# LayerNorm and two matmuls with GELU on one core: three first tiles transposed raw, their mean and deviation applied afterwards

## The chip, the core and the metric

One core of a Trainium2 chip runs the kernel. The metric is the device time of one execution in microseconds (us), median of several runs; the kernel before takes 398.55 us (three runs, 398.34 to 398.63). TensorE (PE) multiplies 128x128 blocks of weights with up to 512 columns and writes to PSUM, eight banks of 512 float columns; VectorE (DVE), ScalarE (ACT) and GpSimd (POOL) work elementwise; the DMA queues used here are issued from SyncE (SP) and ScalarE.

## The reference

```
def _layernorm(x, axis=-1, eps=1e-5):
    m = jnp.mean(x, axis=axis, keepdims=True)
    v = jnp.var(x, axis=axis, keepdims=True)
    return (x - m) / jnp.sqrt(v + eps)

def reference(x, w1, b1, w2, b2):
    y = _layernorm(x, axis=-1)
    h = _gelu(jnp.einsum("bsd,df->bsf", y, w1) + b1)
    return jnp.einsum("bsf,fd->bsd", h, w2) + b2
```

x is (1, 2048, 1024), w1 (1024, 3584), w2 (3584, 1024), all bfloat16; GELU is the tanh form. There is no scale or shift in the normalisation.

## The kernel before

**Tiling.** The 2048 tokens are four blocks of 512, each of four tiles of 128 tokens. A token tile comes with tokens on the partitions; for the first matmul it has to lie the other way (`yT_sb`, 128 features on the partitions, eight of them for 1024 features, index `dt`). The first matmul makes for each of 28 rows of 128 hidden features (index `r`) a PSUM bank of 128x512 from eight matmuls of 512 columns; ScalarE adds b1 and takes GELU into `hT_sb` (`act_gelu`, L430). The second matmul (`out_chunk`, L453) makes 128 tokens x 512 outputs from 28 matmuls; VectorE adds b2 (L477) and SyncE stores. Per block, all 28 rows of the first matmul run, then the eight chunks of the second.

**Order of work.** Each engine's instructions are written out by hand in its own list (`_Prog`), with waits on named events; only VectorE's list behind the head is merged by a small planner at the end (L569 to L584), from due times that are estimates in the source. `ring` (L393) gives the PSUM banks: row 7 uses bank `t`, row 8 the bank of row 0, and so on, so row 8 waits for the GELU of row 0.

**The first block.** Its weights are not there yet: w1's first 896 columns (seven rows) come in eight chunks, one for each `dt`, w0 to w7, mixed with the token tiles in `SP_FIRST_LOADS` (L32) and `ACT_FIRST_LOADS` (L33). So the first seven rows are a "wave": seven banks are open at once (`wave`, L505), and matmuls of 128 columns, one token tile at a time, follow the loads in an order that L508 to L522 write out. TensorE itself transposes the tiles of this block (`pe_T`, L367): a transpose through the identity into bank `t` or a bank not yet in use, then a copy by ScalarE (L385). From block 1 on VectorE transposes (L355).

**Normalising the first block.** VectorE takes batch statistics (L264) and aggregates them (L271); POOL makes 1/deviation by a power (L268). Tiles 2 and 3 are normalised in full ahead of their transposes (L290). Tiles 0 and 1 (`N_CENTRED`) are only centred: tile 0 from a mean that VectorE and ScalarE take half each (L494, L275, L281), tile 1 by L286. Their deviation is applied later to each PSUM bank of this block, 256 columns, by `dve_scale` (L423 to L428), with `rbc_sb`, the two tiles' deviations laid along the columns by sixteen small VectorE transposes (L337).

**Warm-up.** 37 matmuls of a constant (`warm`, L488) run while the first loads come, the last three of them behind tile 0's mean; three more follow its first transposes.

Of the kernel before, what the change touches and what calls it, by code (L numbers as in the profile page):

```python
# [6 lines left out]
ALU = mybir.AluOpType  # L7
# [8 lines left out]
K_GROUPS = 2  # L16
# [4 lines left out]
WARM_A = ((34, None), (3, "m4"))  # L21
WARM_B = 3
N_CENTRED = 2
T_PUTS = {0: (None, None, 6), 1: (21, 35), 2: (96, 118), 3: (140, 156)}
NORM = {0: (0, 2, 8), 1: (0, 4, 8), 2: (0, 4, 8)}
GROUPS_0 = (0, 2, 5, 8)
WAVE_ROWS_0 = 6
WAVE_K = (0, 2, 4, 5, 6, 8)
GROUPS_1 = (0, 4, 8)
W1_CHUNK_COLS = (512, 512, 1024, 640)  # L30
N_W2_CHUNKS = 4
SP_FIRST_LOADS = ("x0a", "w0", "w1", "w2", "w3", "w4", "w5", "x2a", "x2b", "w6", "w7", "x3a", "x3b", "b1", "w8")  # L32
ACT_FIRST_LOADS = ("x0b", "x1")  # L33

T_PE_START = 5.7
T_DVE_START = 16.5
# [54 lines left out]
def bass_standalone__mixer_channel_mlp__prompt_kernel(  # L91
# [22 lines left out]
    nkg = max(1, min(K_GROUPS, DT))  # L114
    KGROUPS = [(h * DT // nkg, (h + 1) * DT // nkg) for h in range(nkg)]
    assert NB1 + NB2 + 1 <= 8 and NB2 == 2
    assert all(c[-1] == DT for c in (*NORM.values(), GROUPS_0, GROUPS_1, WAVE_K))
# [27 lines left out]
    with ExitStack() as es:  # L145
# [19 lines left out]
        half_sb = sb("half_sb", [P, 1], F32)  # L165
        m4_sb = sb("m4_sb", [P, 1], F32)
        rq_sb = sb("rq_sb", [P, N_CENTRED, 32], F32)
        rbc_sb = sb("rbc_sb", [P, N_CENTRED, P], F32)

# [4 lines left out]
        ps_tf = ps_t[:, :, :].bitcast(F32)  # L174

# [37 lines left out]
        def issue(item):  # L213
            if item[0] == "x" and item[-1] in "ab":
                i, h = int(item[1:-1]), "ab".index(item[-1])
                dma(x_sb[:, i, h * HC:(h + 1) * HC], xf[i * P:(i + 1) * P, h * HC:(h + 1) * HC], f"x{i}_{h}",
                    P * HC * 2)
                x_ev[i] = (f"x{i}_0", f"x{i}_1")
            elif item == "b1":
                b1v = b1.rearrange("(t q a) -> q t a", q=4, a=32)  # L220
                for q in range(4):
                    dma(b1r_sb[32 * q:32 * q + FT, :], b1v[q], f"b1{q}", F // 2, waits=["b1z"])
            elif item[0] == "x":
                load_x_tile(int(item[1:]))
            elif item[0] == "w" and int(item[1:]) < len(w1_chunks):
                load_w1(int(item[1:]))
# [32 lines left out]
        pool.op(lambda e: e.memset(b1r_sb[:, :], 0.0), sig="b1z")  # L259
        dve.op(lambda e: e.memset(st_sb[:, :, 12:14], 0.0))  # L260
# [6 lines left out]
        def op_aggr(i):  # L267
            pool.op(lambda e, i=i: e.tensor_tensor(out=rstd_sb[:, i:i + 1], in0=mv_sb[:, i, 1:2],  # L268
                                                   in1=nhalf[:, i:i + 1], op=ALU.pow),
                    waits=[f"mv{i}", "nhalf"], sig=f"rstd{i}")  # L270
# [3 lines left out]
        def op_mean0():  # L274
            return (lambda e: e.tensor_scalar(out=m4_sb[:, :], in0=st_sb[:, 0, 1:2], scalar1=st_sb[:, 0, 4:5],  # L275
                                              scalar2=half_sb[:, :], op0=ALU.add, op1=ALU.add),
                    ["st0_0", "half"], "m4", 0.1)

        def op_norm(i, c0, c1, sig):
            if i == 0:  # L280
                return (lambda e, c0=c0, c1=c1: e.tensor_scalar(  # L281
                            out=o_sb[:, 0, c0:c1], in0=x_sb[:, 0, c0:c1], scalar1=4.0,
                            scalar2=m4_sb[:, :], op0=ALU.mult, op1=ALU.subtract),
                        ["m4"], sig, 0.02 + (c1 - c0) * 0.00055)
            if i < N_CENTRED:
                return (lambda e, i=i, c0=c0, c1=c1: e.tensor_scalar(  # L286
                            out=x_sb[:, i, c0:c1], in0=x_sb[:, i, c0:c1], scalar1=mv_sb[:, i, 0:1],
                            scalar2=None, op0=ALU.subtract),
                        [f"mv{i}"], sig, 0.02 + (c1 - c0) * 0.00055)
# [7 lines left out]
        def ops_norm(i):  # L297
            cuts = NORM.get(i, (0, DT))
# [27 lines left out]
        def ops_rbc():  # L326
            res = []
            for i in range(N_CENTRED):
                res.append((lambda e, i=i: e.tensor_scalar(out=rq_sb[:, i, :], in0=ones[:, 0:32],
                                                           scalar1=rstd_sb[:, i:i + 1], scalar2=(1.0 if i else 0.25),  # L330
                                                           op0=ALU.mult, op1=ALU.mult),
                            ["ones", f"rstd{i}"], f"rq{i}", 0.1))
            for tq in range(4):
                for q in range(4):
                    src = rq_sb[32 * tq:32 * (tq + 1), :, :]
                    dst = rbc_sb[32 * q:32 * (q + 1), :, 32 * tq:32 * (tq + 1)]
                    res.append((lambda e, src=src, dst=dst: e.transpose(out=dst, in_=src), [f"rq{N_CENTRED - 1}"],  # L337
                                ("rbc" if tq == 3 and q == 3 else None), 0.1))
            return res
# [4 lines left out]
        def ops_T(i):  # L344
            blk, t = divmod(i, TPB)
            waits = [y_ev[i][-1]]
            if blk - 2 in mm1_done:
                waits.append(mm1_done[blk - 2])
            res = []
# [15 lines left out]
        t_banks = [("t", ps_t[:, 0, :]), ("2_0", ps_2b[:, 0, :]), ("t", ps_t[:, 0, :])]  # L365

        def pe_T(i, groups, k):  # L367
            blk, t = divmod(i, TPB)
            j0, j1 = groups[k], groups[k + 1]
            bname, bap = t_banks[k if i == 0 else 0]  # L370
            evs = yT_ev.setdefault(i, [None] * DT)
            for j in range(j0, j1):
                waits = []
                if j == j0:
                    waits = ["ident"] + ([bank_read[bname]] if bname in bank_read else [])
                if j == j0 or y_ev[i][j] != y_ev[i][j - 1]:
                    waits.append(y_ev[i][j])
                pe.op(lambda e, i=i, j=j, o=(j - j0) * P, bap=bap: e.transpose(  # L378
                    out=bap[:, o:o + P], in_=(x_sb[:, i] if i else o_sb[:, 0])[:, j * P:(j + 1) * P],
                    identity=ident[:, :]),  # L380
                    waits=waits, sig=(f"tp{i}_{k}" if j == j1 - 1 else None))
                evs[j] = f"te{i}_{k}"
            src = bap[:, 0:(j1 - j0) * P].rearrange("p (j s) -> p j s", j=j1 - j0)
            dst = yT_sb[:, blk % 2, j0:j1, t * P:(t + 1) * P]
            act.op(lambda e, dst=dst, src=src: e.copy(out=dst, in_=src), waits=[f"tp{i}_{k}"], sig=f"te{i}_{k}")  # L385
            bank_read[bname] = f"te{i}_{k}"
            pe_t[0] += (j1 - j0) * 0.056
# [20 lines left out]
        def pe_cell(b, r, t0, t1, bank, waits, sig, dts=None, opens=True, closes=True):  # L408
            n0, n1 = t0 * P, t1 * P
            dts = list(range(DT)) if dts is None else list(dts)  # L410
            waits = list(waits)
            for k, dt in enumerate(dts):
                w = (waits if k == 0 else []) + [f"w1c{w1_chunk_of(r, dt)}"]
                w += [yT_ev[b * TPB + t][dt] for t in range(t0, t1)]
                pe.op(lambda e, b=b, r=r, dt=dt, n0=n0, n1=n1, bank=bank: e.matmul(  # L415
                    unit_bank(bank)[:, n0:n1], lhsT=w1_sb[:, dt, r * P:(r + 1) * P], rhs=yT_sb[:, b % 2, dt, n0:n1],
                    start=(opens and dt == 0), stop=(closes and dt == DT - 1)),
                    waits=w, sig=(sig if dt == DT - 1 else None))
            pe_t[0] += len(dts) * _mm_us(n1 - n0)
            if dts[-1] == DT - 1:  # L420
                est[sig] = pe_t[0]

        def dve_scale(r, bank, wait_ev):  # L423
            ap = unit_bank(bank)[:, 0:N_CENTRED * P]
            crit.append((est[wait_ev], (lambda e, ap=ap: e.tensor_tensor(  # L425
                out=ap, in0=ap, in1=rbc_sb[:, :, :].rearrange("p t s -> p (t s)"), op=ALU.mult),
                [wait_ev, "rbc"], f"sc_{r}", 0.35), 0))
            return f"sc_{r}"  # L428
# [11 lines left out]
        def mm1_row(b, r):  # L440
            bank, uw = new_unit()
            sig = f"m1_{b}_{r}"
            pe_cell(b, r, 0, TPB, bank, uw, sig)
            act_gelu(r, 0, TPB, bank, dve_scale(r, bank, sig) if b == 0 else sig, f"g_{b}_{r}")
# [43 lines left out]
        def warm(n, gate=None):  # L488
            for _ in range(n):
# [4 lines left out]
        act.op(lambda e: e.activation(out=o_sb[:, 1, 0:HC], in_=x_sb[:, 0, HC:D], func=ACT.Copy, scale=2.0 / HC,  # L494
                                      accum_out=half_sb[:, :]), waits=[x_ev[0][1]], sig="half")
        for n, gate in WARM_A:
            warm(n, gate)
        head = [op_stats(0, 0), op_mean0()] + ops_norm(0) + ln_seq([1], ()) + [op_stats(0, 1), op_aggr(0)]
# [129 lines left out]
```

## Time and profile before

| what | us |
|---|---|
| time, median of three runs | 398.55 (398.34 to 398.63) |
| span of the profiled execution, first to last instruction | 396.9 |
| TensorE busy | 394.1 (99%) |
| VectorE busy | 152.8 (38%) |
| ScalarE busy | 82.8 (21%) |
| POOL busy | 9.7 (2%) |
| first useful matmul of the wave starts | 5.92 |
| row 7 of block 0 starts (first matmul of 512 columns) | 20.00 |
| second matmul of block 0, 224 matmuls on the chain | 48.35 |

The profiled execution's own time is not among the runs shown; the page gives its span, and the median lies 1.65 us above it. A row of the profile's timeline reads: start, length, engine, line of the source, operation, output and inputs by the program's names, sizes, count of merged instructions, and in brackets the idle time before it with what ended it. The length of a merged row goes from its first start to its last end; a matmul's modelled end lies some 0.16 us behind the start of the next one, so the spacing of a series is the difference of starts over the count. "PEld" is TensorE's load of weights, beside its matmuls. DMA rows give kilobytes of an issue and the time from issue to landing.

### The profile page before, as it was taken

How to read it: one execution, taken by the hardware profiler on the slowest of the kernel's cores; microseconds unless marked ns; L12 is line 12 of the kernel's file. 1: busy time of each engine (PE TensorE's matmuls, PEld its weight loads, DVE VectorE, ACT ScalarE, POOL GpSimd, SP SyncE). 2: the span in 40 equal slices, each digit the busy share in tenths (PEclk: the TensorE clock that was granted, in tenths of full speed). 3: DMA queues.
4: the chain of work that ended last, by engine and by line, in shares of the span. 5: the costliest groups of instructions: out<-in, count | busy, mean ns of one | idle time of the engine just before them, and what ended most of it. 6: DMA issues, size and time to landing. Idle time of an engine off the chain costs nothing.

```text
span 396.9 us, 4883 instructions
## 1 busy us (share of the span) xinstructions
PE 394.1 (99%) x2116; PEld 191.7 (48%) x2116; DVE 152.8 (38%) x345; ACT 82.8 (21%) x124; POOL 9.7 (2%) x24
## 2 busy tenths in 40 slices
PE   9999999999999999999999999999999999999998
PEld 8944444444444444444444444444444444444447
DVE  5847899989998005988100000001100000001011
ACT  4273430000133442000024433100003334400000
POOL 2101000020002000000000000000000000000000
PEclk9999999999999999999999999999999999999999
DMA  8999940000000000000000000000000000000000
GB/s 286 347 380 384 387 154 13 26 29 13 26 2 0 2 0 1 28 13 26 28 13 0 2 0 2 13 13 28 16 24 15 0 0 2 0 13 28 13 28 26
DMA packets 16924, 23.64 MB, mean 60 GB/s; under 512 B 1672, under 2 KB 10504, under 8 KB 16904
## 3 DMA queue, kind: packets, MB, share of 16 engines
q1 hardware_dynamic: 16616, 22.95, 16.4%
q8 instruction: 16, 0.26, 0.3%
q10 hardware_dynamic: 288, 0.39, 0.3%
q14 instruction: 4, 0.03, 0.0%
HBM read 19.14 MB, written 4.19 MB: 59 GB/s over the span
## 4 chain that ended last, share of the span: by engine, by line
PE 99%; ACT 0%; DVE 0%; issue 0%
PE ps L466 49%; PE ps L415 41%; PE ps_t L415 8%; PE ps L490 1%; PE ps_t L378 0%; ACT yT_sb L385 0%; DVE o_sb L477 0%
## 5 line engine op out<-in xcount | busy, mean ns | idle before, releaser
L466 PE MATMUL ps<-w_sb,hT_sb 128*128 128x512 bf16 (+1 forms) x980 | 194.2, 361 | 0.0
L415 PE MATMUL ps<-yT_sb,w_sb 128*128 128x512 bf16 (+1 forms) x920 | 167.4, 340 | 0.1
L466 PEld LDWEIGHTS ps<-w_sb,hT_sb 128*128 128x128 bf16 x980 | 91.3, 98 | 102.7
L415 PEld LDWEIGHTS ps<-yT_sb,w_sb 128*128 128x128 bf16 x920 | 80.9, 98 | 82.5 <-issue 0.3
L432 ACT ACTIVATE hT_sb<-ps,b_sb 128x512 bf16<-128x512 f32 x94 | 64.0, 688 | 237.2 <-PE ps L415 217.1
L477 DVE TENSOR_TENSOR o_sb<-ps,b_sb 128x512 bf16<-128x512 f32 (+1 forms) x35 | 22.6, 646 | 198.2 <-PE ps L466 198.1
L355 DVE STREAM_TRANSPOSE yT_sb<-x_sb 32x256 bf16<-32x256 bf16 x192 | 83.7, 436 | 26.6 <-PE ps_t L415 23.5
L415 PE MATMUL ps_t<-yT_sb,w_sb 128*128 128x512 bf16 x144 | 34.0, 379 | 0.0
L264 DVE BATCH_NORM_STATS2 st_sb<-x_sb 128x6 f32<-128x512 bf16 x32 | 21.1, 674 | 4.9 <-DMA x_sb<-in_x_dram 4.9
L415 PEld LDWEIGHTS ps_t<-yT_sb,w_sb 128*128 128x128 bf16 x144 | 14.0, 98 | 16.8
L432 ACT ACTIVATE hT_sb<-ps_t,b_sb 128x512 bf16<-128x512 f32 x18 | 12.4, 690 | 17.0 <-PE ps_t L415 14.6
L425 DVE TENSOR_TENSOR ps<-ps,rbc_sb 128x256 f32<-128x256 f32 x24 | 9.7, 426 | 6.1 <-PE ps L415 5.9
L268 POOL TENSOR_TENSOR rstd_sb<-mv_sb,nhalf 128x1 f32<-128x1 f32 x16 | 8.9, 559 | 118.7 <-DVE mv_sb L271 118.7
L290 DVE TENSOR_SCALAR x_sb<-x_sb,mv_sb,rstd_sb 128x1024 bf16<-128x1024 bf16 (+1 forms) x15 | 7.8, 525 | 3.9 <-POOL rstd_sb L268 3.3
L385 ACT COPY yT_sb<-ps_t 128x512 bf16<-128x512 bf16 (+2 forms) x8 | 4.4, 545 | 8.1 <-PE ps_t L378 8.1
L490 PE MATMUL ps<-const-bfloat16-1.0 128*128 128x128 bf16 x40 | 4.6, 302 | 0.8 <-PEq L613 0.8
L490 PEld LDWEIGHTS ps<-const-bfloat16-1.0 128*128 128x128 bf16 x40 | 4.0, 139 | 1.0 <-issue 0.8
L271 DVE BATCH_NORM_AGGREGATE mv_sb<-st_sb 128x2 f32<-128x15 f32 x16 | 3.5, 221 | 1.3
L337 DVE STREAM_TRANSPOSE rbc_sb<-rq_sb 32x64 f32<-32x64 f32 x16 | 3.8, 236 | 0.2
L378 PE MATMUL ps_t<-ident,x_sb 128*128 128x128 bf16 x24 | 2.3, 219 | 0.0
L425 DVE TENSOR_TENSOR ps_t<-ps_t,rbc_sb 128x256 f32<-128x256 f32 x4 | 1.6, 405 | 0.1
L493 ACT ACT_TABLE_LOAD x1 | 1.3, 1283 | 1.7 <-PEq L613 1.7
(24 smaller groups left out, 8.0 us busy)
## 6 DMA issues: line engine op xcount, KB each, us to landing
w_sb<-in_w_dram SPq DMA_DIRECT2D x4, 1792.0 KB, 18.3
out_dram<-o_sb SPq DMA_DIRECT2D x31, 128.0 KB, 1.7
x_sb<-in_x_dram SPq DMA_DIRECT2D x3, 1024.0 KB, 14.1
w_sb<-in_w_dram SPq DMA_DIRECT2D x2, 1024.0 KB, 9.1
w_sb<-in_w_dram SPq DMA_DIRECT2D x1, 2048.0 KB, 15.2
w_sb<-in_w_dram SPq DMA_DIRECT2D x8, 224.0 KB, 4.7
w_sb<-in_w_dram SPq DMA_DIRECT2D x1, 1280.0 KB, 14.7
x_sb<-in_x_dram SPq DMA_DIRECT2D x5, 128.0 KB, 4.6
```

Of the source, the lines that this page charges most:

```text
L264: return (lambda e, i=i, h=h: e.bn_stats(st_sb[:, i, 6 * h:6 * (h + 1)], x_sb[:, i, h * HC:(h + 1) * HC]), [x_ev[i][h]], f"st{i}_{h}", 0.65)
L268: pool.op(lambda e, i=i: e.tensor_tensor(out=rstd_sb[:, i:i + 1], in0=mv_sb[:, i, 1:2], in1=nhalf[:, i:i + 1], op=ALU.pow), waits=[f"mv{i} ...
L290: return (lambda e, i=i, c0=c0, c1=c1: e.tensor_scalar(out=x_sb[:, i, c0:c1], in0=x_sb[:, i, c0:c1], scalar1=mv_sb[:, i, 0:1], scalar2=rst ...
L337: res.append((lambda e, src=src, dst=dst: e.transpose(out=dst, in_=src), [f"rq{N_CENTRED - 1}"], ("rbc" if tq == 3 and q == 3 else None), ...
L355: res.append((lambda e, src=src, dst=dst: e.transpose(out=dst, in_=src), waits, (f"tr{i}" if lastop else None), 0.47))
L385: act.op(lambda e, dst=dst, src=src: e.copy(out=dst, in_=src), waits=[f"tp{i}_{k}"], sig=f"te{i}_{k}")
L415: pe.op(lambda e, b=b, r=r, dt=dt, n0=n0, n1=n1, bank=bank: e.matmul(unit_bank(bank)[:, n0:n1], lhsT=w1_sb[:, dt, r * P:(r + 1) * P], rhs= ...
L425: crit.append((est[wait_ev], (lambda e, ap=ap: e.tensor_tensor(out=ap, in0=ap, in1=rbc_sb[:, :, :].rearrange("p t s -> p (t s)"), op=ALU.m ...
L432: act.op(lambda e, r=r, n0=n0, n1=n1, bank=bank: e.activation(out=hT_sb[:, r, n0:n1], in_=unit_bank(bank)[:, n0:n1], func=ACT.Gelu_apprx_tanh,
L466: pe.op(lambda e, st=st, ft=ft, c0=c0, c1=c1, bank=bank: e.matmul(ps_2[:, bank, 0:c1 - c0], lhsT=hT_sb[:, ft, st * P:(st + 1) * P], rhs=w2 ...
L477: crit.append((est[sig], (lambda e, ob=ob, c0=c0, c1=c1, bank=bank: e.tensor_tensor(out=o_sb[:, ob, c0:c1], in0=ps_2[:, bank, 0:c1 - c0], ...
L490: pe.op(lambda e: e.matmul(ps_1[:, 0, 0:P], lhsT=unit, rhs=unit, start=True, stop=True), waits=[gate] if gate else [])
```

## The change

The changed kernel takes three tiles raw (`N_RAW`) in place of two centred ones:

- The second halves of tiles 0 to 2 come in one load, `xrb`; the first halves in three. The order of the first loads is another. Warm-up is 24 matmuls without a wait.
- TensorE transposes tiles 0 to 2 as they land, in halves, into the *other* half of the double buffer, `yT_sb[:, 1]`. A column of ones stands behind them (column `RC` = 384), so that the wave's matmuls of 385 columns (129 for tile 2 alone) put each row's sum of weights into column 384 of its bank.
- With w the weights, m the mean and s the 1/deviation of a token, the wanted sum over features of w (x - m) s is s times the raw sum, minus m s times the sum of weights. s and -m s of the three tiles are cut into three bfloat16 parts each (`ops_rows`), turned by four VectorE transposes (`ops_rvt`), and spread over all partitions by two matmuls of 384 columns with a selection matrix of ones in three rows (`pe_row`); ScalarE copies the two rows to `row_sb`.
- The seven banks of the wave are corrected in PSUM by two VectorE operations of 385 columns each (`ops_corr`), with the sum of weights from `act_cs`.
- The rows from 7 on need normalised tiles: `ops_fix` multiplies and adds the two rows on the transposed raw tiles, from `yT_sb[:, 1]` to `yT_sb[:, 0]`, tiles 0 and 2 on VectorE, tile 1 on POOL. Row 7 takes tile 3 first and then the three fixed tiles (384 columns). `dve_scale` is gone for all rows.
- Tile 3 is normalised and transposed as before, but into bank `t`, behind the two rows.

The core of the diff:

```
-WARM_A = ((34, None), (3, "m4"))
...
+WARM = 24
+N_RAW = 3
+RC = N_RAW * P
+HALVES = (0, 4, 8)
...
-SP_FIRST_LOADS = ("x0a", "w0", "w1", "w2", "w3", "w4", "w5", "x2a", "x2b", "w6", "w7", "x3a", "x3b", "b1", "w8")
-ACT_FIRST_LOADS = ("x0b", "x1")
+SP_FIRST_LOADS = ("x0a", "w0", "w1", "xrb", "w2", "w3", "w4", "x3a", "x3b", "w5", "w6", "w7", "b1", "w8")
+ACT_FIRST_LOADS = ("x1a", "x2a")
...
+        def ops_rows():
+            return [(lambda e: e.scalar_tensor_tensor(out=rv_sb[:, N_RAW:2 * N_RAW], in0=mv_sb[:, 0:N_RAW, 0],
+                                                      scalar=-1.0, in1=rv_sb[:, 0:N_RAW], op0=ALU.mult, op1=ALU.mult),
+                     ["rstdr"] + [f"mv{i}" for i in range(N_RAW)], "nmr", 0.15),
+                    (lambda e: e.tensor_copy(rv3_sb[:, :, 0], rv_sb[:, :]), ["nmr", "rv0"], "rhi", 0.15),
...
+        def ops_fix(i, tmp, j0, j1, tag, prev):
+            s0, s1 = i * P, (i + 1) * P
+            bc = lambda k: row_sb[:, k:k + 1, s0:s1].to_broadcast([P, j1 - j0, P])
+            return [(lambda e: e.tensor_tensor(out=tmp[:, 0:j1 - j0, :], in0=yT_sb[:, 1, j0:j1, s0:s1], in1=bc(0),
+                                               op=ALU.mult),
+                     ["row0", f"te{i}_0", f"te{i}_1"] + prev, f"fm{i}{tag}", 1.2),
+                    (lambda e: e.tensor_tensor(out=yT_sb[:, 0, j0:j1, s0:s1], in0=tmp[:, 0:j1 - j0, :], in1=bc(1),
+                                               op=ALU.add),
+                     [f"fm{i}{tag}", "row1"], f"fx{i}{tag}", 1.2)]
...
-        def dve_scale(r, bank, wait_ev):
...
+        FX = ["fx0v", "fx1p", "fx2v"]
+        head += ops_fix(0, tmp_sb, 0, DT, "v", []) + ops_fix(2, tmp_sb, 0, DT, "v", ["fx0v"])
+        for fn, waits, sig, _ in ops_fix(1, tmp2_sb, 0, DT, "p", []):
+            pool.op(fn, waits=waits, sig=sig)
+        for o in head:
             dve_put(o)
...
+        def ops_corr(r):
+            ap = unit_bank(wave[r][0])[:, 0:RC + 1]
+            return [(lambda e: e.tensor_tensor(out=ap, in0=ap, in1=row_sb[:, 0, :], op=ALU.mult),
+                     [f"m1_0_{r}", "row0", "row1c"], f"sa_{r}", 0.55),
+                    (lambda e: e.scalar_tensor_tensor(out=ap, in0=row_sb[:, 1, :], scalar=cs_ap[r], in1=ap,
+                                                      op0=ALU.mult, op1=ALU.add),
+                     [f"sa_{r}", cs_ev[r], "row1"], f"sb_{r}", 0.62)]
...
+        def pe_row(k):
+            pe.op(lambda e: e.matmul(ps_tf[:, 0, 0:RC], lhsT=sel_sb[:, :],
+                                     rhs=rvt_sb[:, k * N_RAW:(k + 1) * N_RAW, :].rearrange("p v s -> p (v s)"),
+                                     start=True, stop=True), waits=["sel", "rvt", bank_read["t"]], sig=f"pr{k}")
+            act.op(lambda e: e.copy(out=row_sb[:, k, 0:RC], in_=ps_tf[:, 0, 0:RC]), waits=[f"pr{k}", "row1c"],
+                   sig=f"row{k}")
+            bank_read["t"] = f"row{k}"
...
+        first, most, every = range(NB1), [*range(NB1), R - 1], range(R)
+        pe_T([(0, 0)], "t")
+        pe_T([(1, 0)], "2_0")
+        cells(first, (0,), 0, 1)
+        pe_T([(2, 0)], "2_1")
+        cells(first, (0,), 1, 2)
+        cells((R - 1,), (0,), 0, 2)
+        cells(most, (1,), 0, 2)
+        cells((NB1,), (0, 1), 0, 2)
+        pe_T([(0, 1), (1, 1)], "t")
+        cells(every, (0, 1), 2, 3)
+        cells(every, (2,), 0, 3)
+        pe_T([(2, 1)], "t")
+        cells(every, (3,), 0, 3)
+        cells(first, range(4, DT - 1), 0, 3)
+        pe_row(0)
+        cells(first, (DT - 1,), 0, 3)
+        act_cs(ps_1, 0, NB1, False)
+        last2 = range(NB1, R)
+        cells(last2, (4,), 0, 3)
+        pe_row(1)
+        cells(last2, (5, 6), 0, 3)
+        pe_T([(3, 0), (3, 1)], "t")
+        cells(last2, (DT - 1,), 0, 3)
+        act_cs(ps_2, NB1, R, True)
+        r4 = R // 2 + 1
+        late_cells(3, range(r4), range(h))
+        late_cells(3, range(r4), range(h, DT))
+        late_cells(3, range(r4, R), range(DT))
+        for o in corr:
+            dve_put(o)
...
         def mm1_rows(b, r0):
             for r in range(r0, FT):
-                mm1_row(b, r)
+                mm1_row(b, r, ((N_RAW, TPB), (0, N_RAW)) if b == 0 and r == r0 else ((0, TPB),))
```

`cells(rows, dts, t0, t1)` are the wave's matmuls of these rows and feature blocks over tiles t0 to t1, `late_cells` those of tile 3.

## The prediction

> **What bounds the kernel now.** I read the page first: the share of each engine and the chain of work that ended last.
>
> ```profile
> PE 394.1 (99%) x2116; PEld 191.7 (48%) x2116; DVE 152.8 (38%) x345; ACT 82.8 (21%) x124; POOL 9.7 (2%) x24
> ...
> PE 99%; ACT 0%; DVE 0%; issue 0%
> PE ps L466 49%; PE ps L415 41%; PE ps_t L415 8%; PE ps L490 1%; PE ps_t L378 0%; ACT yT_sb L385 0%; DVE o_sb L477 0%
> ```
>
> TensorE is busy from end to end, so an edit counts only through what it makes TensorE do or wait for. The timeline of TensorE shows where that can be (start, length, engine, line, instructions).
>
> ```profile
> 0.82 4.26 PE L490 MATMUL ps<-const-bfloat16-1.0 128*128 128x128 bf16 x37 [0.82 <-PEq L613]
> ...
> 5.92 0.49 PE L415 MATMUL ps<-yT_sb,w_sb 128*128 128x128 bf16 x6
> ...
> 8.55 3.57 PE L415 MATMUL ps<-yT_sb,w_sb 128*128 128x128 bf16 x61
> ...
> 16.20 3.96 PE L415 MATMUL ps<-yT_sb,w_sb 128*128 128x128 bf16 x68
> ...
> 20.00 1.89 PE L415 MATMUL ps_t<-yT_sb,w_sb 128*128 128x512 bf16 x8
> ```
>
> The first useful matmul starts at 5.92, the wave of seven rows follows almost without a gap, and row 7 starts at 20.00. Of one group it is the spacing that counts, not its length: 61 matmuls of 128 columns in 3.45 us are 56 ns each, and 512 columns go at 216 ns (40 in 8.63 on the chain), so a matmul costs 2.5 ns and 0.417 ns a column. The 37 at the start are spaced 107 ns, half that speed, until about 5.3. Everything behind row 7 is the same program in both kernels. So the forecast is: when does row 7, and then row 8, start in the changed kernel, against 20.00 and 21.76?
>
> **The start.** Normalising tile 0 ahead of its transposes (L494, L275, L281) goes; raw tiles are transposed as they land. Tile 0's first half lands at 3.2 (issued 0.78, 2.4 us). The 24 warm matmuls left end at 0.9 + 24 x 0.107 = 3.4; four transposes at the slow spacing and 0.2 of drain give 4.1; the copy of 128x512 takes 585 ns, the hand-over 0.12 (5.77 to 5.89 today): first useful matmul at 4.80, **1.1 us earlier**, with 8 transposes done instead of 5.
>
> **TensorE's own work from there.** 10 matmuls of 128 columns, 9 of 256, 14 of 129, 42 of 385 and 56 of 128: 0.56 + 0.98 + 0.79 + 6.84 + 3.13 = 12.30, where 224 of 128 columns cost 12.5. With 24 transposes (1.34) and two row broadcasts of 384 columns (0.33): 13.97. About 9 instructions before 5.3 run at half speed: 0.27. Ends for that: 0 and 0.9, if full speed came at 7.0.
>
> **Loads.** The order changes, the bytes up to the last first chunk of w1 do not. Today the third chunk (issued 2.15, 4.2 to 4.7 us) is in at 6.7 with 1184 KB ahead of and in it; the changed kernel has its one load of three second halves complete at 1216 KB: 6.3 to 6.8, I take 6.6. Chunk 2 comes at 7.3 and is needed at 8.1, chunks 5, 6 and 7 at 9.9, 10.5, 11.1 and are needed at 11.4, 12.2 and 13.4. TensorE waits for none of them. The chunk of row 7 lands at 16.6 and stays hidden; SyncE's and ScalarE's queues have no new wait ahead of a load.
>
> **VectorE's path to the rows.** It waits for 6.6, then three statistics (spaced 0.61) to 8.5, three aggregates to 9.1; POOL's power (0.55) is covered by tile 3's statistics and aggregate to 10.65. The five small dependent steps on 3 or 6 columns are not in this profile; the nearest rows are 180 to 273 ns, so 0.23 each with the hand-over: 11.8. Four transposes of 32x192: between 236 ns (32x64) and 436 (32x256), 0.37: **13.3**. TensorE reaches the first row broadcast at 13.23, so it stalls 0.2 (0 at 6.3, 0.4 at 6.8). All TensorE work stands behind that wait.
>
> **Bank t is now also the rows' bank.** Row 0 copied (128x384, 480 ns) at 14.3; row 1 computed at 14.75, copied at 15.6; tile 3's transposes wait for it, 0.13. After them only two matmuls (0.33) are left, while the copy of tile 3's first half ends 0.85 after the last transposes of that tile began to drain: TensorE waits 0.58 there, where today no such wait shows. With 0.07 for tile 1's copy: 1.0 of stalls.
>
> Sum: 4.80 + 13.97 + 0.27 + 1.0 and 0.15 in single waits = **20.2** for row 7, against 20.00. The earlier start is spent.
>
> **The fix of the raw tiles, which row 7 waits for.** Row 7 first does tile 3 (8 x 56 ns), then needs all of FX at 20.64. Each raw tile takes a multiply and an add over 128x1024 with one float input. VectorE does tiles 0 and 2: 292 ns for 128 columns and 692 for 512 (L477) give 1.04 ns a column, so 1.2 for 1024, four times, from row 0's copy at 14.33. POOL does tile 1, an operation that the trace does not show. Its rows:
>
> ```profile
> 0.78 0.20 POOL L254 MEMSET ones<- 128x128 bf16 x1 [0.29 <-POOLq L613]
> 1.05 0.29 POOL L255 TENSOR_SCALAR_AFFINE_SELECT ident<-ones 128x128 bf16<-128x128 bf16 x1
> 1.29 0.11 POOL L258 MEMSET nhalf<- 128x16 f32 x1
> ...
> 6.78 0.72 POOL L268 TENSOR_TENSOR rstd_sb<-mv_sb,nhalf 128x1 f32<-128x1 f32 x1 [5.32 <-DVE mv_sb L271]
> 8.29 0.55 POOL L268 TENSOR_TENSOR rstd_sb<-mv_sb,nhalf 128x1 f32<-128x1 f32 x1 [0.78 <-DVE mv_sb L271]
> ```
>
> Bounds for one pass of 1024: the memsets grow 0.82 ns a column, 0.94 us; the select, which reads a tile and writes one, takes 292 ns for 128, so 2.3 us; two inputs at its whole price, 4.7. I take 2.3, the nearest row. [...]
>
> Side by side, VectorE is done at 14.33 + 4.8 = 19.2 and POOL at 14.4 + 4.6 + 0.1 = 19.1, both before 20.64: nothing lost. But the trace speaks against side by side. The first of POOL's powers took 0.72; the twelve from 33.2 on are all alike:
>
> ```profile
> L268 POOL TENSOR_TENSOR rstd_sb<-mv_sb,nhalf x12: 547/548/549, 33.2 to 128.5; 128x1 f32<-128x1 f32 x12
> ```
>
> ```profile
> 6.73 0.62 DVE L286 TENSOR_SCALAR x_sb<-x_sb,mv_sb 128x512 bf16<-128x512 bf16 x2
> ```
>
> The slow one is the only one that ran during VectorE's fast centring of 128x512, which moves 512 columns in 0.35 us; those beside batch statistics, or beside L425 with PSUM as one input, took 548. That is one case, and also the first power of the run, so it is weak. [...]
>
> **Forecast: they take turns.** Then the six passes follow one another, whichever begins: 14.33 + 4 x 1.2 + 2 x 2.3 = 23.75, and row 7's second part starts at 23.9, 3.25 late. VectorE's seven corrections are queued behind its last fix: row 0's two (385 columns from PSUM: 385/960 + 0.15 = 0.56 by L425's 426 ns for 256) end at 24.8, its gelu (0.69) at 25.55, and row 8, which takes over row 0's bank, starts at 25.65, where row 7 would be done at 25.2: 0.45 more. The next rows ask for one gelu per 1.73 and get one per 1.1. Row 8 at 25.65 against 21.76: **+3.9**. The 21 scalings of later rows (L425, 0.43 each) that disappear were off the path: each now delays only a gelu that has 1 us to spare.
>
> The profiled span is 396.9; nothing behind row 8 changes, so 400.8. The median of the runs, 398.55, lies 1.65 above this span, for what lies outside it; with the same 1.65: **402.4**. By POOL's price: 2 x price more or less, so 401.4 at 1.8, 403.8 at 3.0, 399.7 at 0.94 and 407.2 at 4.7.
>
> **Rivals.**
> 1. Not slower: the engines run side by side, FX is ready at 19.2, and only the sum of TensorE's waits decides: +0.2 (0.05 to 0.4 by the load), 398.7. For it: most powers ran undisturbed beside VectorE. It decides as long as one pass of POOL stays under 3.1 us.
> 2. Side by side and the head start partly kept: of 1.0 us of stalls most vanish (copies end earlier, the rows come before 13.2): -0.8 or better, 397.7. Against it: the copy's 585 ns stand in six rows.
> 3. Side by side, but POOL alone needs 4.7: 14.4 + 9.4 + 0.1 = 23.9, a stall of 3.35, and the corrections come in time: 0.2 + 3.35, 402.1.
> 4. The clock. Slow spacing ends at about 5.3 today, and useful work begins after it; in the changed kernel it begins before. If full speed came at 7.0: 0.6 more than rival 1, 399.4. [...]
>
> **Chances.** Taking turns 0.54, rival 1 0.26, rival 2 0.12, rivals 3 and 4 0.04 each. About 0.2%, 0.8 us, is what a measurement of this kernel tells from no change. Faster by more: rival 2, 0.12. Within: rival 1 and half of rival 4, 0.28. Slower: the rest, 0.60. The forecast's own range, POOL at 1.8 to 3.0, is 401.4 to 403.8; to hold 8 in 10 the range reaches down over rival 1: 398.3 to 403.8.
>
> **What would show it.** First useful matmul near 4.8 and row 7 near 20.2 show the start right. Turns show as fixes on VectorE and passes on POOL that never overlap, or as rows much longer than 1.2 and 2.3 where they do, and as a stall of about 3 us between the parts of row 7. If row 7's parts adjoin, the forecast is wrong and rival 1 or 2 holds. A stall of 0.6 ahead of tile 3's first matmuls, and 0.2 at the first row, test the rest.

## The result, and the profile after

The changed kernel takes 401.85 us (median of four runs, 401.23 to 402.67) against 398.53 of the kernel before beside it (398.34 to 398.63): 1.0085 times as long, with a 95% interval of 1.007 to 1.0101. Five further executions of the same kernel (below) gave 401.32 against 398.37, 1.0074 [1.0062, 1.0087]. It is slower by about 3 us, and the question is where a kernel that starts its useful work 1.1 us earlier loses 4.

First the page of the changed kernel: the granted clock in 40 slices of 10 us (9 stands for 90% of full speed or more), and the chain of work that ended last, its shares of the span by engine and by line.

```profile
PEclk9989999999999999999999999999999999999999
...
PE 97%; DVE 2%; ACT 0%; issue 0%; DVEq 0%
PE ps L476 48%; PE ps L424 40%; PE ps_t L424 8%; DVE yT_sb L348 1%; DVE o_sb L345 1%; PE ps L500 1%; PE ps_t L392 0%; ACT yT_sb L400 0%; ACT row_sb L571 0%; PE ps L392 0%; PE ps_t L568 0%; DVE o_sb L487 0%; DVEq L72 0%
```

TensorE's share of the chain has gone from 99% to 97%, and the two lines of the fix on VectorE, L345 and L348, have come into it with 1% each: 2% of 401 is some 8 us that the chain runs through VectorE instead of TensorE. And one slice of the clock, 20 to 30 us, shows 8 where before no late slice did. TensorE's timeline (start, length, engine, line, instructions, in brackets the idle time before and what ended it) shows both:

```profile
4.78 0.71 PE L424 MATMUL ps<-yT_sb,w_sb 128*128 128x128 bf16 x5 [0.25 <-ACT yT_sb L400]
...
13.44 0.33 PE L568 MATMUL ps_t<-rvt_sb,sel_sb 128*128 128x384 bf16 x1
...
16.94 3.30 PE L424 MATMUL ps<-yT_sb,w_sb 128*128 128x128 bf16 x56 [0.35 <-ACT yT_sb L400]
20.08 0.61 PE L424 MATMUL ps_t<-yT_sb,w_sb 128*128 128x128 bf16 x8
22.96 2.40 PE L424 MATMUL ps_t<-yT_sb,w_sb 128*128 128x384 bf16 x8 [2.28 <-DVE yT_sb L348]
25.16 5.04 PE L424 MATMUL ps<-yT_sb,w_sb 128*128 128x512 bf16 x19
```

The kernel before has its row 8 here:

```profile
21.73 4.48 PE L415 MATMUL ps<-yT_sb,w_sb 128*128 128x512 bf16 x20
```

The first useful matmul is at 4.78 (before: 5.92), row 7 at 20.08 (before: 20.00). Between the two parts of row 7 TensorE stands still until VectorE's last fix (L348). Row 8 starts at 25.16 instead of 21.73, 3.43 later. The eight matmuls of 384 columns then take 2.20 from start to next start, 275 ns each, where the 22 of 385 columns from 9.84 on, at full speed, went at 163. Now VectorE's, POOL's and (for the GELU of row 0) ScalarE's timelines of the same execution:

```profile
14.31 1.23 DVE L345 TENSOR_TENSOR o_sb<-yT_sb,row_sb 128x1024 f32<-128x1024 bf16 x1
15.69 2.93 DVE L348 TENSOR_TENSOR yT_sb<-o_sb,row_sb 128x1024 bf16<-128x1024 f32 x1 [0.15 <-ACT row_sb L571]
18.65 2.91 DVE L345 TENSOR_TENSOR o_sb<-yT_sb,row_sb 128x1024 f32<-128x1024 bf16 x1
21.59 1.22 DVE L348 TENSOR_TENSOR yT_sb<-o_sb,row_sb 128x1024 bf16<-128x1024 f32 x1
...
23.33 0.62 DVE L552 SCALAR_TENSOR_TENSOR ps<-row_sb,cs_sb,ps 128x385 f32<-128x385 f32 x1
```

```profile
14.36 3.18 POOL L345 TENSOR_TENSOR tmp_sb<-yT_sb,row_sb 128x1024 f32<-128x1024 bf16 x1 [2.88 <-ACT row_sb L571]
17.61 2.86 POOL L348 TENSOR_TENSOR yT_sb<-tmp_sb,row_sb 128x1024 bf16<-128x1024 f32 x1
```

```profile
23.99 0.69 ACT L433 ACTIVATE hT_sb<-ps,b_sb 128x512 bf16<-128x512 f32 x1 [6.55 <-DVE ps L552]
```

The same operation takes 1.22 or 2.93 on VectorE. The long ones are those that lie beside a pass of POOL, and the ends interlock. POOL's first row starts 0.05 after VectorE's first and ends at 17.54; VectorE's second ends at 18.62, POOL's second at 20.47, VectorE's third at 21.56. Read as turns, the ends follow one another by 1.23 (VectorE), 2.00 (POOL), 1.08 (VectorE), 1.85 (POOL), 1.09 (VectorE), and then 1.25 for the last pass, alone: 8.5 in all, from 14.31 to 22.81. On this reading a row shows an instruction from its start, the time in which it is kept waiting included; the experiment on VectorE's fixes alone (below) bears that out.

Last, one stretch of the windows view of the changed kernel (stretch, its length, then the busy time and count of each engine, the granted clock, DMA share, GB/s):

```profile
23.30:26.70 3.40, 3.40 (x11) 1.46 (x10) 3.27 (x6) 1.83 (x3) 0.00 (x0) 0.50 1.07 371
```

Just after the stall, for 3.4 us, TensorE was granted half its clock (0.50; 1.00 and 0.99 in the stretches 22.90:23.30 and 26.70:28.00 beside it). By the trace's record of the clock the stretch goes from 23.32 to 26.73. Behind row 8's start 1.57 of it are left, worth 0.78 of lost work. 3.43 + 0.78 = 4.2, and the spans differ by 401.1 - 396.9 = 4.2: this execution is accounted for.

### The profile page after: what moved, and what is told of

Same layout as the page of the kernel before. It is cut to its first block, busy times and chain, and to the rows that moved or that the text cites. A ratio compares the mean times of both kernels' runs of the same rounds, so it can differ in the third digit from the quotient of the medians.

```text
span 401.1 us, 4669 instructions
## 1 busy us (share of the span) xinstructions
PE 395.6 (99%) x2017; PEld 188.8 (47%) x2017; DVE 154.2 (38%) x320; ACT 83.3 (21%) x125; POOL 16.0 (4%) x30
## 4 chain that ended last, share of the span: by engine, by line
PE 97%; DVE 2%; ACT 0%; issue 0%; DVEq 0%
PE ps L476 48%; PE ps L424 40%; PE ps_t L424 8%; DVE yT_sb L348 1%; DVE o_sb L345 1%; PE ps L500 1%; PE ps_t L392 0%; ACT yT_sb L400 0%; ACT row_sb L571 0%; PE ps L392 0%; PE ps_t L568 0%; DVE o_sb L487 0%; DVEq L72 0%
## 5 line engine op out<-in xcount | busy, mean ns | idle before, releaser
L424 PE MATMUL ps<-yT_sb,w_sb 128*128 128x512 bf16 (+4 forms) x827 | 168.5, 362 | 0.6 <-ACT yT_sb L400 0.6
L424 PE MATMUL ps_t<-yT_sb,w_sb 128*128 128x512 bf16 (+2 forms) x152 | 35.2, 376 | 2.3 <-DVE yT_sb L348 2.3
L301 DVE TENSOR_SCALAR x_sb<-x_sb,mv_sb,rstd_sb 128x1024 bf16<-128x1024 bf16 x13 | 7.1, 545 | 2.8 <-POOL rstd_sb L278 2.0
L552 DVE SCALAR_TENSOR_TENSOR ps<-row_sb,cs_sb,ps 128x385 f32<-128x385 f32 x7 | 4.4, 624 | 0.2
L348 DVE TENSOR_TENSOR yT_sb<-o_sb,row_sb 128x1024 bf16<-128x1024 f32 x2 | 4.2, 2076 | 0.2 <-ACT row_sb L571 0.2
L400 ACT COPY yT_sb<-ps_t 128x512 bf16<-128x512 bf16 x6 | 3.3, 587 | 4.3 <-PE ps_t L392 4.3
L345 DVE TENSOR_TENSOR o_sb<-yT_sb,row_sb 128x1024 f32<-128x1024 bf16 x2 | 4.1, 2066 | 0.2
L550 DVE TENSOR_TENSOR ps<-ps,row_sb 128x385 f32<-128x385 f32 x7 | 3.9, 559 | 0.0
L345 POOL TENSOR_TENSOR tmp_sb<-yT_sb,row_sb 128x1024 f32<-128x1024 bf16 x1 | 3.2, 3180 | 2.9 <-ACT row_sb L571 2.9
L348 POOL TENSOR_TENSOR yT_sb<-tmp_sb,row_sb 128x1024 bf16<-128x1024 f32 x1 | 2.9, 2862 | 0.1
```

The costliest lines, as they stand in the source:

```text
L301: return (lambda e, i=i, c0=c0, c1=c1: e.tensor_scalar(out=x_sb[:, i, c0:c1], in0=x_sb[:, i, c0:c1], scalar1=mv_sb[:, i, 0:1], scalar2=rst ...
L345: return [(lambda e: e.tensor_tensor(out=tmp[:, 0:j1 - j0, :], in0=yT_sb[:, 1, j0:j1, s0:s1], in1=bc(0), op=ALU.mult), ["row0", f"te{i}_0" ...
L348: (lambda e: e.tensor_tensor(out=yT_sb[:, 0, j0:j1, s0:s1], in0=tmp[:, 0:j1 - j0, :], in1=bc(1), op=ALU.add), [f"fm{i}{tag}", "row1"], f"f ...
L424: pe.op(lambda e: e.matmul(unit_bank(bank)[:, n0:n1], lhsT=w1_sb[:, dt, r * P:(r + 1) * P], rhs=yT_sb[:, buf, dt, n0:n1], start=start, sto ...
L552: (lambda e: e.scalar_tensor_tensor(out=ap, in0=row_sb[:, 1, :], scalar=cs_ap[r], in1=ap, op0=ALU.mult, op1=ALU.add), [f"sa_{r}", cs_ev[r] ...
```

## The experiments

The theory: VectorE's and POOL's fixes exclude each other, so six passes run in turn and row 7's second part waits for their sum; a fall of the clock behind the idle time is added in some executions. The rivals: the passes are slow for another reason (POOL's own price, any work on VectorE), or the time is lost in the new order of the first block.

**All fixes on VectorE.** If the engines take turns, moving POOL's passes to VectorE makes the chain of passes shorter, not longer.

```
-        FX = ["fx0v", "fx1p", "fx2v"]
-        head += ops_fix(0, tmp_sb, 0, DT, "v", []) + ops_fix(2, tmp_sb, 0, DT, "v", ["fx0v"])
-        for fn, waits, sig, _ in ops_fix(1, tmp2_sb, 0, DT, "p", []):
-            pool.op(fn, waits=waits, sig=sig)
+        FX = ["fx0v", "fx1v", "fx2v"]
+        head += ops_fix(0, tmp_sb, 0, DT, "v", []) + ops_fix(1, tmp_sb, 0, DT, "v", ["fx0v"])
+        head += ops_fix(2, tmp_sb, 0, DT, "v", ["fx1v"])
```

> Tile 1's fix moves from POOL to VectorE, between those of tiles 0 and 2; nothing else changes. Turns (the long rows of the changed kernel are waiting for the other engine): all six VectorE rows of the fix take 1.2 to 1.25 us, the last ends at 14.3 + 6 x 1.24 = 21.75 instead of 22.81, row 7's second part starts at about 21.9, the gelu of row 0 ends at 23.6 and row 8 starts at 23.7: 2.0 over before, about 400.5. Rival (VectorE's second and third pass are slow of themselves, 2.9 us, because of their operands): rows of 2.9 stay, the last fix ends after 24 and the time is over 402.5.

Measured: 400.46 (four runs, 400.05 to 400.78) against 398.40, ratio 1.005 [1.0037, 1.0064]. Two lines of its VectorE timeline and two of TensorE's:

```profile
15.95 1.23 DVE L348 TENSOR_TENSOR yT_sb<-o_sb,row_sb 128x1024 bf16<-128x1024 f32 x1 [0.15 <-ACT row_sb L570]
...
20.99 1.22 DVE L348 TENSOR_TENSOR yT_sb<-o_sb,row_sb 128x1024 bf16<-128x1024 f32 x1
```

```profile
22.36 1.46 PE L424 MATMUL ps_t<-yT_sb,w_sb 128*128 128x384 bf16 x8 [1.41 <-DVE yT_sb L348]
24.12 2.12 PE L424 MATMUL ps<-yT_sb,w_sb 128*128 128x512 bf16 x9 [0.31 <-ACT hT_sb L433]
```

All six passes take 1.22 or 1.23, and the last ends at 22.21, earlier than with POOL's help (22.81) although the first began 0.26 later. (Expected were 21.75 for that end and 23.7 for row 8, which starts at 24.12.) Taking the helper away makes the kernel 0.8 to 1.4 us faster (against 401.31, where the clock did not fall, and 401.85). Row 8 now also waits 0.31 for row 0's GELU.

**The fixes cut to one eighth, everywhere.** Fixes of one feature block of eight; the other seven are zeros for the three raw tiles in rows 7 to 27, so this part of the computation is left out. All else of the changed first block stays.

```
+        pool.op(lambda e: e.memset(yT_sb[:, 0, 1:DT, 0:RC], 0.0), sig="yz")
...
-        head += ops_fix(0, tmp_sb, 0, DT, "v", []) + ops_fix(2, tmp_sb, 0, DT, "v", ["fx0v"])
-        for fn, waits, sig, _ in ops_fix(1, tmp2_sb, 0, DT, "p", []):
+        head += ops_fix(0, tmp_sb, 0, 1, "v", ["yz"]) + ops_fix(2, tmp_sb, 0, 1, "v", ["fx0v"])
+        for fn, waits, sig, _ in ops_fix(1, tmp2_sb, 0, 1, "p", []):
```

> The six passes of the fix are cut to one of eight feature blocks; the other seven blocks of the three tiles are zeros for rows 7 to 27. Theory: without the wait for the fix only TensorE's own path is left, row 7's two parts adjoin, row 7 starts at 20.1 and row 8 at 21.9: 0.1 to 0.4 over before, 398.6 to 399.0. Rival (the start itself costs more than the fix): 399.5 or more. Rival (the earlier start is worth its 1.1 us): under 397.8.

Measured: 398.34 (eleven runs, 397.91 to 398.64) against 398.40, ratio 0.9998 [0.9989, 1.0007]. Its TensorE timeline:

```profile
20.08 1.91 PE L425 MATMUL ps_t<-yT_sb,w_sb 128*128 128x128 bf16 x16
21.83 2.54 PE L425 MATMUL ps<-yT_sb,w_sb 128*128 128x512 bf16 x11
```

Row 7 starts at 20.08 exactly as in the changed kernel, its two parts adjoin (16 matmuls in one row), and row 8 follows at 21.83. So the whole loss is the fixes, and the rest of the change neither costs nor gains anything measurable. That second half is as instructive as the first: three tiles less normalised ahead, a start 1.1 us earlier, and no scaling of the later rows are together worth nothing here.

**Only VectorE's fixes cut.** POOL does tile 1 whole; VectorE's fixes of tiles 0 and 2 are one eighth, the rest zeros for these two tiles in rows 7 to 27.

```
+        pool.op(lambda e: e.memset(yT_sb[:, 0, 1:DT, 0:P], 0.0), sig="yz")
+        pool.op(lambda e: e.memset(yT_sb[:, 0, 1:DT, 2 * P:RC], 0.0), sig="yz2")
...
-        head += ops_fix(0, tmp_sb, 0, DT, "v", []) + ops_fix(2, tmp_sb, 0, DT, "v", ["fx0v"])
+        head += ops_fix(0, tmp_sb, 0, 1, "v", ["yz2"]) + ops_fix(2, tmp_sb, 0, 1, "v", ["fx0v"])
```

> VectorE's four passes are cut to one of eight feature blocks (the others are zeros), POOL's two passes on tile 1 stay whole. Turns: with VectorE nearly out of the way POOL's rows fall from 3.18 and 2.86 to about 2.0 and 1.9, done by 18.5. Rival (POOL is that slow by itself): 3.2 and 2.9 stay, done by 20.5. The time is that of the kernel with all fixes cut in both cases, since both are before 20.6.

Measured: 398.55 (one run), row 8 at 22.11. VectorE's timeline, then POOL's:

```profile
14.59 0.29 DVE L347 TENSOR_TENSOR o_sb<-yT_sb,row_sb 128x128 f32<-128x128 bf16 x1
15.97 1.06 DVE L350 TENSOR_TENSOR yT_sb<-o_sb,row_sb 128x128 bf16<-128x128 f32 x1 [1.08 <-ACT row_sb L573]
17.06 2.04 DVE L347 TENSOR_TENSOR o_sb<-yT_sb,row_sb 128x128 f32<-128x128 bf16 x1
```

```profile
14.64 2.24 POOL L347 TENSOR_TENSOR tmp_sb<-yT_sb,row_sb 128x1024 f32<-128x1024 bf16 x1 [2.86 <-ACT row_sb L573]
16.96 2.00 POOL L350 TENSOR_TENSOR yT_sb<-tmp_sb,row_sb 128x1024 bf16<-128x1024 f32 x1
```

This is the clearest view of the turns. A pass of 128 columns that takes 0.29 takes 1.06 when it starts at 15.97, and 2.04 when it starts at 17.06: it ends at 17.03 and 19.10, each 0.15 after the end of POOL's row (16.88, 18.96). It doesn't run slower beside POOL; it waits out POOL's whole instruction. With little in its way POOL takes 2.24 (with the wait for VectorE's first short pass, which ends at 14.88, 2.00 before POOL's row does) and 2.00, so POOL alone is neither 0.94 nor 4.7.

Not every pair of rows does this. In the changed kernel POOL's power on one column of tile 3 and a VectorE subtraction on six columns, both inputs in SBUF, lie over each other:

```profile
10.92 0.56 POOL L278 TENSOR_TENSOR rstd_sb<-mv_sb,nhalf 128x1 f32<-128x1 f32 x1 [0.63 <-DVE rv_sb L285]
```

```profile
11.12 0.17 DVE L289 TENSOR_TENSOR rr_sb<-rv_sb 128x6 f32<-128x6 f32 x1
```

The subtraction ends at 11.29, POOL's row at 11.48. The next one of its kind (L292), behind POOL's row, takes no less: 0.18. So this pair doesn't wait out a whole row. The waiting is shown here for passes of 128 columns and more; whether and how long so short a power holds VectorE off stays open.

**POOL behind VectorE's fixes.** The same work, but POOL's passes lie beside VectorE's corrections (one input in PSUM, one in SBUF) instead of its fixes (both in SBUF). It tells "any work of VectorE" from "this kind of work".

```
-        for fn, waits, sig, _ in ops_fix(1, tmp2_sb, 0, DT, "p", []):
+        for fn, waits, sig, _ in ops_fix(1, tmp2_sb, 0, DT, "p", ["fx2v"]):
```

> POOL's fix of tile 1 waits for VectorE's last fix, so that POOL's two passes run beside VectorE's corrections (one input in PSUM, one in SBUF) in place of its fixes (both inputs in SBUF). All work is done. Theory (only VectorE work with two SBUF inputs takes turns with POOL): the four VectorE fixes take 1.23 each and end near 19.7; POOL's rows are 2.24 and 2.0 as beside short fixes, and end near 24.0; the correction rows beside them stay at 0.56 and 0.62; row 7's second part starts near 24.1, row 8 follows near 25.4 without waiting for a GELU; TensorE idles some 3.4 in one piece, so half speed behind it is likely: 401.6 to 403. Rival (any work of VectorE takes turns with POOL): corrections stretch to about 2 or POOL's rows to about 3, FX comes at 25.5 or later and row 8 at 26.8 or later, 403 to 405.

Measured: 402.12 (one run) against 398.36. VectorE, POOL and TensorE:

```profile
18.70 1.23 DVE L348 TENSOR_TENSOR yT_sb<-o_sb,row_sb 128x1024 bf16<-128x1024 f32 x1
...
20.44 0.62 DVE L552 SCALAR_TENSOR_TENSOR ps<-row_sb,cs_sb,ps 128x385 f32<-128x385 f32 x1
20.97 0.56 DVE L550 TENSOR_TENSOR ps<-ps,row_sb 128x385 f32<-128x385 f32 x1
```

```profile
20.07 2.13 POOL L345 TENSOR_TENSOR tmp_sb<-yT_sb,row_sb 128x1024 f32<-128x1024 bf16 x1 [8.08 <-DVE yT_sb L348]
22.28 2.00 POOL L348 TENSOR_TENSOR yT_sb<-tmp_sb,row_sb 128x1024 bf16<-128x1024 f32 x1
```

```profile
24.39 1.46 PE L424 MATMUL ps_t<-yT_sb,w_sb 128*128 128x384 bf16 x8 [3.21 <-DVE ps L550]
```

The corrections stay at 0.56 and 0.62, as in the kernel with all fixes on VectorE, where POOL has none, and POOL takes 2.13 and 2.00: with one input of VectorE's work in PSUM neither held the other up here. (The corrections also write to PSUM, where the fixes write to SBUF; no run here changes the inputs and leaves the output, so which of the two frees them is not shown.) Both this order and the changed kernel run all the passes; in turns they end at 22.81, one set wholly behind the other at 24.28, from a start 0.49 later. (The profile names L550 as what ended TensorE's wait, but POOL's row that ends at 24.28 is the one that matters: the event it names is only the last one seen.) The clock did not fall, against expectation (mean 1.000), though TensorE idled 3.21.

**The stall filled.** 38 matmuls of 128 columns with zero weights between the two parts of row 7, so that TensorE is busy while it waits; they add zeros to row 7's bank.

```
+                for _ in range(FILL if k else 0):
+                    pe.op(lambda e: e.matmul(unit_bank(bank)[:, 0:P], lhsT=z_sb[:, :], rhs=unit, start=False,
+                                             stop=False, skip_group_check=True), waits=["z0"])
```

> The changed kernel, with 38 matmuls of 128 columns on a tile of zeros between the two parts of row 7, some 2.1 us of the 2.3 that TensorE stands still; they add nothing. Theory (the idle time halves the clock in some executions): the granted clock is 1.000 in every run and the median 401.2 to 401.4, that of the changed kernel's two runs at clock 1.000. Rival (the halved clock has another cause): 0.996 and 402.4 to 402.7 in about half of the runs, as now.

> The 38 matmuls of zero weights between row 7's parts again, for more executions beside the unaltered kernel's. Theory: every execution has a mean clock above 0.998 and stays below 402.0. Rival (the fall of the clock has nothing to do with the idle time): executions with 0.996 and 402.3 or more occur as often as in the unaltered kernel beside it.

> The changed kernel once more, unaltered, for more executions of it. Theory (in some executions the idle time ahead of row 7's second part lets the clock fall to half for one stretch of some 3.4): its times fall into two groups that go with the granted clock, near 401.2 to 401.5 with a mean clock of 1.000, and near 402.3 to 402.7 with 0.996, and nothing between the two without a reason in the clock. Rival (401.2 to 402.7 is plain scatter): times spread without regard to the clock.

Measured: 401.53 (401.02 to 401.74) the first time, 401.19 (400.88 to 401.54) the second, mean clock 1.000 in all ten. The unaltered kernel beside the second: 401.32 (401.22 to 401.76), mean clock 1.000 in all five. TensorE's timeline of the first filled execution, then of the unaltered kernel's repetition:

```profile
20.79 2.36 PE L454 MATMUL ps_t<-const-bfloat16-1.0,z_sb 128*128 128x128 bf16 x38
23.23 1.46 PE L427 MATMUL ps_t<-yT_sb,w_sb 128*128 128x384 bf16 x8
```

```profile
23.37 1.46 PE L424 MATMUL ps_t<-yT_sb,w_sb 128*128 128x384 bf16 x8 [2.28 <-DVE yT_sb L348]
```

Of the nine executions of the changed kernel, the two with a mean clock of 0.996 took 402.38 and 402.67, the seven with 1.000 took 401.22 to 401.76 (median 401.31). So time and clock go together, and a fall is worth 1.1 to 1.4 us; in the profiled one it is 0.78 behind row 8, and about 0.4 before, where row 8 would have followed row 0's GELU (ended 24.68) at some 24.76. But the second half of the theory, that filling prevents it, is supported and not shown: none in ten against two in nine could be chance, and the repetition had the same stall of 2.28 and no fall. The two medians of the filled kernel also lie on both sides of 401.31: without a fall, filling is worth nothing. The scatter was wider than expected: 401.58 and 401.76 of the repetition lie above the 401.2 to 401.5 of full clock. The one of 401.76 is the profiled one: there VectorE waits 0.73 for the load of tile 3, the first row broadcast starts at 13.85 instead of 13.44, and row 7 at 20.48 instead of 20.08, so that some 0.4 us of scatter come from a load and not from the clock.

**Two raw tiles in place of three.** What if only as many tiles are raw as VectorE can fix in time? Tile 2 is normalised in full and comes in by transposes of its own like tile 3, with its load in halves on SyncE; the order of the wave is adapted.

```
-N_RAW = 3
+N_RAW = 2
...
-SP_FIRST_LOADS = ("x0a", "w0", "w1", "xrb", "w2", "w3", "w4", "x3a", "x3b", "w5", "w6", "w7", "b1", "w8")
-ACT_FIRST_LOADS = ("x1a", "x2a")
+SP_FIRST_LOADS = ("x0a", "w0", "w1", "xrb", "w2", "w3", "x2a", "x2b", "w4", "w5", "w6", "w7", "x3a", "x3b", "b1", "w8")
+ACT_FIRST_LOADS = ("x1a",)
...
-        FX = ["fx0v", "fx1p", "fx2v"]
+        FX = ["fx0v", "fx1v"]
...
+        head += ops_fix(0, tmp_sb, 0, DT, "v", []) + ops_fix(1, tmp_sb, 0, DT, "v", ["fx0v"])
```

> Two tiles raw in place of three, both fixed by VectorE alone; tile 2 is normalised in full, as tile 3 is, with its load in halves again, and the matmuls of both follow in the wave as their transposes come; all work is done. Theory (the loss of the changed kernel is the fixes' length behind row 0's copy and nothing else): four fixes of 1.23 from about 14.5 end at 19.5, ahead of row 7; its two parts adjoin; row 8 starts between 21.55 and 21.85, against 21.73 of the kernel before: 398.1 to 398.6, the same as before within 0.1%. Rival (the order of the first block itself costs, by waits for loads, for single transposes and for two more bank hand-overs): row 8 after 22.2, 399 or more.

Measured: 398.50 (eleven runs, 398.04 to 399.23) against 398.36, ratio 1.0004 [0.9995, 1.0013]. Two lines of VectorE's timeline, two of TensorE's:

```profile
14.68 0.55 DVE L301 TENSOR_SCALAR x_sb<-x_sb,mv_sb,rstd_sb 128x1024 bf16<-128x1024 bf16 x1 [0.25 <-POOL rstd_sb L278]
...
18.91 1.23 DVE L348 TENSOR_TENSOR yT_sb<-o_sb,row_sb 128x1024 bf16<-128x1024 f32 x1
```

```profile
20.06 1.91 PE L424 MATMUL ps_t<-yT_sb,w_sb 128*128 128x256 bf16 x16
21.80 3.40 PE L424 MATMUL ps<-yT_sb,w_sb 128*128 128x512 bf16 x15
```

The last fix ends at 20.14, 0.6 later than expected. Row 0 was copied at 14.53, as expected, but on VectorE the normalising of tile 3 (L301) stands ahead, after a wait for POOL's power, so that the first fix starts at 15.14. The last one is still ahead of row 7's second part; the parts adjoin and row 8 starts at 21.80. Four passes fit in front of row 7, six don't. The loss is gone, and nothing is gained over the kernel before: this version ties with it, and none of the versions measured here that do all the work is faster than the kernel before.

## Why the prediction was right, and where it was not

**The start: right.** First useful matmul at 4.78 (4.80 forecast), row 7 at 20.08 (20.2 forecast). The sum's parts were less exact than the sum. The load of the three second halves was in at 7.04, outside its bounds of 6.3 to 6.8; over the profiled executions of these variants it ranged from 6.7 to 7.5. Behind it the three aggregates took 0.36 together instead of 0.6, and VectorE's five small steps 1.01 instead of 1.15, so the rows were there at 13.28 as forecast (13.3): errors that cancel, and so partly luck. The wait of 0.2 ahead of the first row broadcast did not show: the 22 matmuls from 9.84 at 163 ns end at 13.43, and the broadcast starts at 13.44. The stall ahead of tile 3's matmuls is 0.51 (two matmuls of 0.165 from 16.10, the next at 16.94) against 0.58. Three slips in the working change nothing that counts: 0.9 + 24 x 0.107 is 3.5 and not 3.4 (the 4.1 behind it is right), 14.33 + 4 x 1.2 + 2 x 2.3 is 23.73, and rival 3's stall, 23.9 less 20.64, is 3.26 and not 3.35.

**The clock at the start: a rival that mattered little.** Full speed came at 6.25 in the changed kernel and at 4.71 in the one with all fixes cut; both started the first row broadcast at 13.44, since VectorE's rows set that moment in the second (in the first TensorE came there at the same time). It isn't always so: with all fixes on VectorE the rows were there at 13.19, but TensorE came to the broadcast only at 13.69. Its 14 matmuls of 128 and 256 columns ahead of tiles 0 and 1's second transposes had taken 1.79, against 1.53 in the changed kernel, and that is where the 0.26 of that run come from (this profile has no record of the clock; the slower spacing is all that it shows). No run shows the 7.0 that the sum's upper end and rival 4 took for full speed: it was the author's estimate, and in the profiles whose record is told here full speed came at 6.25 at the latest, in the kernel before at 5.34.

**Turns: right, and shown.** The prediction rested on one slow POOL power of 0.72; from that row to whole passes that take turns was the author's estimate, and no row of the kernel before shows it. The doubt it names, that this was also the first power of its run, can be met: the first powers of these kernels take 0.71 on two columns (two raw tiles) and 0.88 on three, on one line with the 0.55 of a later one on one column, so being first shows no cost there. The three experiments above carry it now: without POOL six passes take 1.22 or 1.23 each, a short pass of 0.29 takes 2.04 and ends 0.14 behind POOL's row, and corrections with an input in PSUM stay at 0.56 and 0.62 beside POOL. Rival 1, side by side, is out for that reason; the price it gave, 398.7, is near what the kernel costs when the fixes are cut (398.34). Rival 2, faster by a kept head start, is out by the same run. Rival 3, POOL alone at 4.7, is out by POOL's 2.24 and 2.00.

**The price of a pass: the term that was mis-sized.** Forecast were four of 1.2 and two of 2.3, 9.4 in all; in turns they took 1.23, 1.08, 1.09 and 1.25 on VectorE and 2.00 and 1.85 on POOL: 8.5. A pass that waited is about 0.15 shorter, counted from its turn, than one that did not (1.08 and 1.09 against 1.23, 1.85 against 2.00); where those 0.15 are won no run shows. The nearest row for POOL, the select of 128 columns at 292 ns, gave 2.3, and the wide bounds of 0.94 and 4.7 were not needed: beside the corrections, where nothing was in the way, POOL took 2.13 and 2.00.

**Row 8: +3.43 in the profiled execution against +3.9.** With fixes 0.94 earlier at their end, row 0's corrections end at 23.95 (24.8 forecast) and its GELU at 24.68 (25.55). At full speed row 8 would have followed at about 24.76, some 3.0 late; the rest of the 3.43 is the clock.

**The clock behind the stall: missed.** The forecast priced the stall as idle time only. In the profiled execution the clock was also halved behind it, for 3.41 us; the mean clock of 0.996 says the same of one more of the nine. Rival 4 looked for the clock at the start alone.

**From span to time: 1.65 was too much.** In the changed kernel's profiled execution the time is 1.28 above the span (402.38 against 401.1), and in the runs of the kernel before it is about 1.3. So the forecast of 402.4 met that execution's 402.38 by errors that cancel, which is luck: -0.87 for the passes (row 8 some 3.03 late at full speed, against 3.9), +1.18 for the clock (about 0.4 ahead of row 8 and 0.78 behind it), -0.37 for the time outside the span. Against the median of 401.85, and 401.31 where the clock stays up, it is 0.5 to 1.1 too high.

## What to carry to other kernels

Before work is shared between VectorE and POOL, look at the operands: here, where VectorE's passes had both inputs in SBUF, POOL's were added to them instead of lying beside them (four and two in turns ended at 22.81), and VectorE alone was faster (all six ended at 22.21); beside VectorE's work in PSUM neither engine was held up (0.56 and 0.62, and 2.13 and 2.00). A step taken out ahead of the bound engine is worth only what the next wait leaves of it: 1.1 us of earlier start ended in the wait for the two rows. And a stall of some 2 us on TensorE may cost more than its length, if the clock falls behind it: the two of nine executions with a mean clock of 0.996 were 1.1 to 1.4 us longer than the others' median.

## What the runs showed of the hardware that was not expected

In the profiles with a record of the clock its changes lie 3.413 us, or a multiple of it, apart. In the changed kernel's profile full speed was granted at 6.25, taken back at 23.32 and granted again at 26.73: 17.07 and 3.41 later, five times and once 3.413. The stretches at full speed of the other profiles with such a record fit too: 392.53 (the kernel before, both runs with fixes cut) and 395.95 (POOL behind the fixes, both repetitions) are 115 and 116 times 3.413. On the same raster the stall from 20.53 to 22.96 falls whole into the stretch from 19.90 to 23.32. In the repetition, full speed from 4.74 puts a boundary at 21.80, which splits the stall (20.93 to 23.37) into 0.9 and 1.6; with POOL behind the fixes, full speed from 5.86 puts one at 22.92, which splits the idle time from 21.02 to 24.39 into 1.9 and 1.5. Neither fell. So the one stall with a fall behind it lay 2.43 within one stretch of 3.41, and the two without a fall 1.6 and 1.9 at most; three profiles suggest that this decides and don't prove it. If the raster's place is chance, an estimate from these figures is that a stall of 2.43 lies whole in one stretch in (3.41 - 2.43) / 3.41, 29% of the executions; two of nine fit that.

A power on three columns took POOL 0.88, on two 0.71, where one column takes 0.55.
